# The product state @ w_in in another grouping: four batches in float32, four in high and low parts, each head in its own 64 rows of the array

## The chip, the cores and the metric

One core of a Trainium2 chip runs the kernel. The metric is the device time of one execution in microseconds (us). The engines meant below: PE (TensorE, matmuls; PEld its weight loads), DVE (VectorE), ACT (ScalarE), POOL (GpSimd) and SP (SyncE, whose queue issues the DMAs here). Each engine takes its instructions strictly in the order in which they stand.

## The reference

Softmax attention in both directions between x (8 batches, 8 heads, 512 tokens, 64 dims) and a small state (32 rows a head), then for all 8 x 544 rows a product, h - tanh(h), and a second product:

```python
scores = scale * x @ state.T;  a = softmax(scores);   xread = a @ state
scores2 = scale * state @ x.T; a2 = softmax(scores2); sread = a2 @ x
rows = concat([xread, sread], axis=tokens)      # (8 * 544, 512)
h = rows @ w_in                                 # w_in 512 x 2048
out = (h - tanh(h)) @ w_out                     # w_out 2048 x 512
```

The weights come as 8-byte floats and are made float32 on the chip.

## The kernel before

xread @ w_in is computed as a @ M with M = state @ w_in, per batch and head 32 x 2048 numbers. M is made on the chip, in four quarters q of w_in's columns (512 each), by pairs of heads p = 0 to 3 (one block of 128 rows of w_in).

The large products go through float32r: an operand is split exactly into hi + lo (`split`: ACT writes hi, DVE or POOL writes lo), and hi*hi + hi*lo + lo*hi are added up. A plain float32 matmul needs no split; in the trace it shows as two records.

The work goes by chunks: chunk i is batch i (512 tokens) for i < 8, chunk 8 holds the rows of sread. In a chunk, `hidden(f)` makes one of 16 column blocks of h (tile hps, from a's parts aT and M's parts m), then t = h - tanh(h) and g, the two parts of t; `output(f)` adds g's block into four output banks (tile ops; 12 matmuls a block, lines 393 to 395). `hidden` runs two blocks ahead of `output`. `load_m(b, q)` fetches a quarter of M (tile mr) and splits it into m.

M is made in three ways:

- `m_first_two(q, p)`, batches 0 and 1: one float32 matmul over all 128 rows. The two heads of a pair are laid out as a block matrix with zero halves (input sp, tile sps), so that one matmul gives both. Batch 0's part is copied straight into the tile mr, batch 1's goes to DRAM (tiles st, md).
- `m_units(0)`, batches 2 to 5: w's head of 64 rows is split, its hi stacked over its lo (tile wst, 64 rows each), and two float32r matmuls per head give all three products (state's lo and hi, each given twice, input sm).
- `m_units(1)`, batches 6 and 7: one matmul per head, with state's hi in half of the columns and its lo in the other half (input sl); two addends go to DRAM, and load_m adds them (tile ml).

The first quarter of batches 0 and 1 is made in a start sequence of its own, written out by hand. In the first chunk the float64 weights are converted as well (`convert_win`, `convert_wout`: DVE's lines 119 and 120, ACT's 122, POOL's 123), and the second batch's softmax is made.

The order on each engine is set by a scheduler that works on the program as written. What stands beside what in the program is set by the table SCH: for each kind of work (conversions "conv", m_first_two "pair", attention "att", m_units "m0", "m1", w_out "wo") the step (16 per chunk) at which each unit is written. PSUM banks for M, scores and transposes are two (pool ps_a). The raw tile mr has one buffer.

Of the kernel before, what the change touches and what calls it, by code (L numbers as in the profile page):

```python
# [31 lines left out]
def attention_ffn(ctx: ExitStack, tc: tile.TileContext, xT, xn, bd, sp, sm, sl, win, wout, xout, sout):  # L32
# [36 lines left out]
    # state @ w_in, [half of the heads, head, row, column]; of the last two batches, two addends  # L69
    mdram = [  # L70
        [[dram.tile([2, 4, NS, 512], F32, name=f"md{b}{q}{i}") for i in range(1 if b < 6 else 2)] for q in range(NQ)]
        for b in range(B)
    ]
# [13 lines left out]
    def split(hi, lo, src, sub=None):  # L87
        """src = hi + lo."""
        nc.scalar.copy(hi, src)  # L89
        return (sub or nc.vector).tensor_sub(lo, src, hi)  # L90

    class Weight:
        """A [P, 512] part of a weight: load() issues its load, convert() makes float32 of it."""
# [16 lines left out]
        def steps(self, dst):  # L110
            """convert() by engines: Vector's first and second part, Scalar's, GpSimd's."""
            if self.src.dtype == F32:
# [5 lines left out]
                # sign, the exponent's top bit; its other seven bits, 20 bits of the fraction  # L118
                lambda: nc.vector.tensor_scalar(u, high, 3, 0x3FFFFFFF, ALU.logical_shift_left, ALU.bitwise_and),  # L119
# [21 lines left out]
    def m_first_two(q, p):  # L141
        """Heads 2p and 2p + 1 of the first two batches, in float32 as it stands."""
        k, c = p // 2, p % 2
        if p == 0:
            # The first batch's part stays on chip.
            m_first[q] = pool.tile([P, 2, 512], F32, tag="mr", name=f"mr0{q}", bufs=RRB)
        ps = bank(ps_a, f"mps0{q}{p}")
        nc.tensor.matmul(ps, sps[:, p], wfs[q, k][:, c], start=True, stop=True)
        nc.scalar.copy(m_first[q][64 * c : 64 * c + 64, k], ps[0:64])
        stage = pool.tile([P, 2, 512], F32, tag="stage", name=f"st0{q}{p}", bufs=SB)  # L150
        nc.scalar.copy(stage[64:128, 0], ps[64:128])
# [4 lines left out]
    def m_units(g):
        """Of the next four batches (g = 0) and of the last two (g = 1), by pairs of heads.

        The columns of the last two batches' product: half of them by the state's hi, half by its lo.
        """  # L160
        raw = pool.tile([P, H, P], F32, tag="stage", name=f"smr{g}", bufs=SB)
        s = pool.tile([P, 2, H, P], F32R, tag="sm", name=f"sms{g}", bufs=1)
        if g == 0:
            nc.sync.dma_start(raw, sm)
            split(s[:, 0], s[:, 1], raw)
        else:
            nc.sync.dma_start(raw[:, :, 0:64], sl)
            split(s[:, 0, :, 0:64], s[:, 0, :, 64:128], raw[:, :, 0:64])
        for q in range(NQ):
            for k in range(2):  # L170
                w = pool.tile([P, 2, 512], F32, tag="wf", name=f"w1{g}{q}{k}", bufs=WB)
                nc.sync.dma_start(w, wf[q][:, 2 * k : 2 * k + 2])
                for c in range(2):
                    p = 2 * k + c
                    # Even heads: hi over lo; odd heads: lo over hi.
                    t = twins(f"wst{g}{q}{p}", [P, 2, 512], F32R)
                    split(t[0:64, 0], t[64:128, 0], w[0:64, c], WSUB)
                    split(t[64:128, 1], t[0:64, 1], w[64:128, c], WSUB)
                    hs = slice(2 * c, 2 * c + 2)
                    stage = pool.tile([P, 2, 512], F32, tag="stage", name=f"st{g}{q}{p}", bufs=SB)  # L180
                    for e in range(2):
                        h = 2 * p + e
                        ps = bank(ps_a, f"mps{g}{q}{h}")
                        if g == 0:
                            nc.tensor.matmul(ps, s[:, 1, h], t[:, e], start=True, stop=False)  # L185
                        nc.tensor.matmul(ps, s[:, 0, h], t[:, e], start=(g == 1), stop=True)  # L186
                        nc.scalar.copy(stage[:, e], ps)  # L187
# [517 lines left out]
```

## Time and profile before

| | |
|---|---|
| device time, median of 3 runs | 701.36 us (699.81 to 701.6) |
| span of the profiled execution, first to last instruction | 699.7 us; no other time of that execution is given |
| PE busy | 670.6 us (96%) |
| DVE busy | 464.8 us (66%) |
| ACT busy | 378.4 us (54%) |
| DMA moved | 99.68 MB, 142 GB/s over the span |

PE's busy share alone says little, since matmuls overlap at their ends: a float32r matmul is recorded at some 0.39 us while the next starts 0.23 us after it. What counts is the distance between starts, and whether PE waits.

### The profile page before, as it was taken

Reading aid. Unit: us, or ns where it says so; the run is one execution under the profiler, and the core shown is the slowest. Engines: PE = TensorE matmul, PEld = TensorE weight load, DVE = VectorE, ACT = ScalarE, POOL = GpSimd, SP = SyncE. Lnnn points to the kernel's source line nnn. Section 1 sums busy time; section 2 is a strip of 40 time slices with the busy share of each in tenths; the row PEclk is TensorE's granted clock in tenths of the full one; section 3 lists DMA queues with packets and bytes.
Section 4 is the critical chain, followed back from the end, with each engine's and each line's share of the span. In section 5 each row is a group of like instructions: output and inputs, shape, how many; then the busy total and the mean of one; then the engine's idle time right before and its main releaser. Section 6 shows DMA issues by size and latency. Waiting matters only on the chain.

```text
span 699.7 us, 8842 instructions
## 1 busy us (share of the span) xinstructions
PE 670.6 (96%) x3146; PEld 530.2 (76%) x3146; DVE 464.8 (66%) x755; ACT 378.4 (54%) x663; POOL 79.2 (11%) x59
## 2 busy tenths in 40 slices
PE   5888995999999999999999999999999999999997
PEld 2555663888778887888788878887888788888896
DVE  5998899965695559556776558545864596444442
ACT  3876866566674655447656545543543354333442
POOL 3766656200000000000000000000000000000000
PEclk9989899899999999999999999999999999999999
DMA  8887762553554554245635632563241312001400
GB/s 298 291 298 273 250 248 100 186 199 111 152 168 141 164 163 128 90 151 151 186 120 163 170 99 65 177 189 111 77 173 61 112 69 91 30 1 38 143 31 31
DMA packets 46316, 99.68 MB, mean 142 GB/s; under 512 B 6208, under 2 KB 12096, under 8 KB 46272
## 3 DMA queue, kind: packets, MB, share of 16 engines
q1 hardware_dynamic: 46272, 99.11, 43.9%
q8 instruction: 25, 0.41, 0.3%
q14 instruction: 19, 0.16, 0.1%
HBM read 67.11 MB, written 31.98 MB: 142 GB/s over the span
## 4 chain that ended last, share of the span: by engine, by line
PE 84%; DVE 9%; ACT 2%; issue 2%; POOL 1%; DMA 1%; SPq 0%; ACTq 0%; DVEq 0%; POOLq 0%
PE ops L395 17%; PE ops L393 17%; PE ops L394 16%; PE hps L356 9%; PE hps L355 9%; PE hps L357 8%; PE rps L309 2%; PE mps L186 2%; DVE w L120 2%; PE sps L249 2%; PE mps L185 1%; DMA w01d<-in_win 1%; PE pps L301 1%; DVE wor L119 1%; DVE w L119 1%
## 5 line engine op out<-in xcount | busy, mean ns | idle before, releaser
L393 PE MATMUL ops<-wo,g 128*128 128x512 f32 x544 | 211.1, 398 | 4.8 <-ACT wo L89 2.9
L394 PE MATMUL ops<-wo,g 128*128 128x512 f32 x544 | 215.1, 395 | 0.2 <-POOL wo L90 0.2
L395 PE MATMUL ops<-wo,g 128*128 128x512 f32 x544 | 208.9, 394 | 0.0
L363 ACT ACTIVATE t<-hps 128x512 f32<-128x512 f32 (+1 forms) x142 | 81.3, 573 | 151.3 <-PE hps L357 150.7
L363 DVE TENSOR_TENSOR t<-hps,t 128x512 f32<-128x512 f32 (+1 forms) x142 | 93.2, 658 | 102.3 <-ACT t L363 101.3
L393 PEld LDWEIGHTS ops<-wo,g 128*128 128x128 f32 x544 | 103.0, 190 | 32.7 <-ACT wo L89 4.6
L90 DVE TENSOR_TENSOR g<-t,g 128x512 fp32r<-128x512 f32 (+1 forms) x142 | 100.2, 706 | 39.9 <-ACT g L89 37.9
L89 ACT CAST g<-t 128x512 fp32r<-128x512 f32 (+1 forms) x142 | 84.7, 596 | 72.7 <-DVE t L363 69.8
L394 PEld LDWEIGHTS ops<-wo,g 128*128 128x128 f32 x544 | 103.0, 189 | 23.3 <-issue 2.3
L395 PEld LDWEIGHTS ops<-wo,g 128*128 128x128 f32 x544 | 103.4, 190 | 22.5 <-issue 0.5
L355 PE MATMUL hps<-aT,m 128*128 128x512 f32 x248 | 99.5, 402 | 3.3 <-DVE t L363 1.7
L357 PE MATMUL hps<-aT,m 128*128 128x512 f32 x248 | 98.4, 399 | 0.7 <-DVE m L90 0.7
L356 PE MATMUL hps<-aT,m 128*128 128x512 f32 x248 | 98.5, 398 | 0.0
L355 PEld LDWEIGHTS hps<-aT,m 128*128 128x128 f32 x248 | 47.3, 191 | 15.3 <-ACT m L89 2.4
L90 DVE TENSOR_TENSOR wst<-w,wst 64x512 fp32r<-64x512 f32 x64 | 46.0, 718 | 19.2 <-ACT wst L89 15.9
L356 PEld LDWEIGHTS hps<-aT,m 128*128 128x128 f32 x248 | 47.5, 191 | 11.7 <-issue 2.2
L357 PEld LDWEIGHTS hps<-aT,m 128*128 128x128 f32 x248 | 47.4, 191 | 11.7 <-DVE m L90 1.5
L90 DVE TENSOR_TENSOR m<-mr,m 128x1024 fp32r<-128x1024 f32 x31 | 39.9, 1287 | 9.4 <-ACT m L89 9.3
L187 ACT COPY st<-mps 128x512 f32<-128x512 f32 x64 | 36.7, 587 | 14.6 <-PE mps L186 14.3
L89 ACT CAST wst<-w 64x512 fp32r<-64x512 f32 x64 | 39.6, 619 | 2.3 <-issue 1.5
L89 ACT CAST m<-mr 128x1024 fp32r<-128x1024 f32 x31 | 32.3, 1042 | 3.6 <-DMA mr<-md 3.4
L90 POOL TENSOR_TENSOR wo<-wor,wo 128x512 fp32r<-128x512 f32 x16 | 25.3, 1586 | 6.0 <-ACT wo L89 6.0
(216 smaller groups left out, 661.7 us busy)
## 6 DMA issues: line engine op xcount, KB each, us to landing
md<-st SPq DMA_DIRECT2D x144, 128.0 KB, 2.3
mr<-md SPq DMA_DIRECT2D x28, 512.0 KB, 4.0
xT<-in_xT SPq DMA_DIRECT2D x16, 512.0 KB, 4.4
xn<-in_xn SPq DMA_DIRECT2D x16, 512.0 KB, 4.8
w<-wf SPq DMA_DIRECT2D x16, 512.0 KB, 4.9
out_x<-ob SPq DMA_DIRECT2D x32, 256.0 KB, 2.2
wn<-wf SPq DMA_DIRECT2D x8, 512.0 KB, 3.9
ml<-md SPq DMA_DIRECT2D x8, 512.0 KB, 3.6
```

The costliest lines, as they stand in the source:

```text
L89: nc.scalar.copy(hi, src)
L90: return (sub or nc.vector).tensor_sub(lo, src, hi)
L119: lambda: nc.vector.tensor_scalar(u, high, 3, 0x3FFFFFFF, ALU.logical_shift_left, ALU.bitwise_and),
L120: lambda: nc.vector.scalar_tensor_tensor(u, high, 0xC0000000, u, ALU.bitwise_and, ALU.bitwise_or),
L187: nc.scalar.copy(stage[:, e], ps)
L355: nc.tensor.matmul(ps, mhi[k][:, cols], ahi[:, k], start=(k == 0), stop=False)
L356: nc.tensor.matmul(ps, mhi[k][:, cols], alo[:, k], start=False, stop=False)
L357: nc.tensor.matmul(ps, mlo[k][:, cols], ahi[:, k], start=False, stop=(k == nk - 1))
L363: tanhs.append((nc.scalar.activation(t, ps, AF.Tanh).ins, nc.vector.tensor_sub(t, ps, t).ins))
L393: nc.tensor.matmul(o, g[:, 0, tok], wo[:, f, 0], start=(f == 0), stop=False)
L394: nc.tensor.matmul(o, g[:, 0, tok], wo[:, f, 1], start=False, stop=False)
L395: return nc.tensor.matmul(o, g[:, 1, tok], wo[:, f, 0], start=False, stop=(f == NFF - 1)).ins
```

## The change

Batches 0 to 3 now go through `m_first_four`: for each pair of heads two float32 matmuls, each over the 64 rows of its own head (rows 0 to 63 and 64 to 127 of the array), into two banks, with the four batches' 128 state rows as columns (input sf, second half of the tile sps). All of M goes through DRAM, batch 0's too; only the first quarter keeps its old way (batches 0 and 1 by the block matrix). Batches 2 and 3 of that first quarter, and batches 4 to 7 of all quarters, go through one `m_units`: w's 128 rows are split at once (one ACT and one DVE operation for a pair of heads), and each head gets three float32r matmuls over its 64 rows. Each pair's results leave in one write per batch (`pairs_out`). The two lists "m0", "m1" become one list "m".

```diff
-    def m_first_two(q, p):
...
-        ps = bank(ps_a, f"mps0{q}{p}")
-        nc.tensor.matmul(ps, sps[:, p], wfs[q, k][:, c], start=True, stop=True)
-        nc.scalar.copy(m_first[q][64 * c : 64 * c + 64, k], ps[0:64])
...
-        nc.sync.dma_start(mdram[1][q][0][k, 2 * c : 2 * c + 2].rearrange("h n f -> (h n) f"), stage[64:128, 0])
+    def pairs_out(q, p, ps, batches, name):
+        k, hs = p // 2, slice(2 * (p % 2), 2 * (p % 2) + 2)
+        n = NS * len(batches)
+        stage = pool.tile([P, 2, 512], F32, tag="stage", name=f"st{name}{q}{p}", bufs=SB)
+        for e in range(2):
+            nc.scalar.copy(stage[:n, e], ps[e][:n])
+        for j, b in enumerate(batches):
+            nc.sync.dma_start(mdram[b][q][k, hs].rearrange("h n f -> n h f"), stage[NS * j : NS * j + NS])
+
+    def m_first_four(q, p):
+        ps = [bank(ps_a, f"mps0{q}{p}{e}") for e in range(2)]
+        for e in range(2):
+            rs = slice(64 * e, 64 * e + 64)
+            nc.tensor.matmul(ps[e], sps[rs, 1, p], wfs[q, p // 2][rs, p % 2], start=True, stop=True)
+        pairs_out(q, p, ps, range(4), "f")

-    def m_units(g):
...
-                    split(t[0:64, 0], t[64:128, 0], w[0:64, c], WSUB)
-                    split(t[64:128, 1], t[0:64, 1], w[64:128, c], WSUB)
...
-                        if g == 0:
-                            nc.tensor.matmul(ps, s[:, 1, h], t[:, e], start=True, stop=False)
-                        nc.tensor.matmul(ps, s[:, 0, h], t[:, e], start=(g == 1), stop=True)
+    def m_units():
...
+        for batches in (range(2, 4), range(4, 8)):
...
+            for q in range(1 if n < P else NQ):
...
+                        split(t[:, 0], t[:, 1], w[:, c], WSUB)
+                        ps = [bank(ps_a, f"mps{n}{q}{p}{e}") for e in range(2)]
+                        for i, (x, y) in enumerate(((1, 0), (0, 1), (0, 0))):
+                            for e in range(2):
+                                rs = slice(64 * e, 64 * e + 64)
+                                nc.tensor.matmul(
+                                    ps[e][:n], s[rs, x, p, cols], t[rs, y], start=(i == 0), stop=(i == 2)
+                                )
+                        pairs_out(q, p, ps, batches, f"g{n}")

     def load_m(b, q):
-        if b == 0:
-            r = m_first[q]
...
-                nc.vector.tensor_add(r, r, r2)
+        r = pool.tile([P, 2, 512], F32, tag="mr", name=f"mr{b}{q}", bufs=RRB)
+        nc.sync.dma_start(r, mdram[b][q].rearrange("g h n f -> (h n) g f"))
...
-    SCH = ... "m0": [11, 11, 15, 15, 20, 21, ..., 35, 36], "m1": [40, 46, 52, ..., 79, 84], ...
+    SCH = ... "m": [9, 10, 11, 13, 34, 35, ..., 52, 54], ...
```

In the order of instructions the change shows at three places. The lines of the changed file stand 15 to 17 lower: its L154 is the float32 matmul of m_first_four, L178 the float32r one of m_units, L338 to L340 are `hidden`, L376 to L378 `output`, L346 makes t, L87 is split's subtraction, L116 and L117 are the conversions.

First, PE in the first chunk, where its second quarter (hps0_4, q = 1) begins. Before (mps02.. are pairs of q = 2):

```order
L394 MATMUL ops0_3_392<-wo_77,g0_2_345 128x512
L395 MATMUL ops0_3_392<-wo_77,g0_2_345 128x512
L355 MATMUL hps0_4_497<-aT0_124,m01_494 128x512
L356 MATMUL hps0_4_497<-aT0_124,m01_494 128x512
L355 MATMUL hps0_5_548<-aT0_124,m01_494 128x512
L356 MATMUL hps0_5_548<-aT0_124,m01_494 128x512
L148 MATMUL mps020_562<-w020_468,sps_126 128x512
```

After, at the same place (behind g0_2), and then where hps0_4 now stands:

```order
L377 MATMUL ops0_3_399<-wo_77,g0_2_347 128x512
L378 MATMUL ops0_3_399<-wo_77,g0_2_347 128x512
L154 MATMUL mps0131_440<-w011_323,sps_118 128x512
L284 MATMUL pps01_461<-ident_72,s01_154 128x128 x4
L154 MATMUL mps0200_575<-w020_480,sps_118 128x512
L154 MATMUL mps0201_576<-w020_480,sps_118 128x512
L376 MATMUL ops0_0_396<-wo_77,g0_3_436 128x512
```

```order
L154 MATMUL mps0220_597<-w021_536,sps_118 128x512
L154 MATMUL mps0221_598<-w021_536,sps_118 128x512
L154 MATMUL mps0230_608<-w021_536,sps_118 128x512
L154 MATMUL mps0231_609<-w021_536,sps_118 128x512
L338 MATMUL hps0_4_511<-aT0_116,m01_508 128x512
```

The last half that hps0_4's quarter needs (mps0131, pair 3 of q = 1) stands behind g0_2's products, and hps0_4 moved behind all four pairs of the next quarter.

Second, DVE in the first chunk, where the third quarter's t and g come (t0_8, g0_8). Before:

```order
L120 SCALAR_TENSOR_TENSOR wor6_663<-wo6d_611,wor6_663 128x512
L119 TENSOR_SCALAR wor7_723<-wo7d_619 128x512
L363 TENSOR_TENSOR t0_8_743<-hps0_8_736,t0_8_743 128x512
L363 TENSOR_TENSOR t0_9_792<-hps0_9_785,t0_9_792 128x512
L120 SCALAR_TENSOR_TENSOR wor7_723<-wo7d_619,wor7_723 128x512
L90 TENSOR_TENSOR g0_8_746<-t0_8_743,g0_8_746 128x512
```

After (wst6400 and wst6401 are the first units of batches 2 and 3, e10 and at10 the second batch's softmax):

```order
L87 TENSOR_TENSOR wst6400_1011<-w16400_1009,wst6400_1011 128x512
L257 TENSOR_TENSOR e10_739<-e10_739,z10_869 128x512
L87 TENSOR_TENSOR wst6401_1073<-w16400_1009,wst6401_1073 128x512
L346 TENSOR_TENSOR t0_8_787<-hps0_8_780,t0_8_787 128x512
L259 STREAM_TRANSPOSE at10_874<-e10_739 128x512
L116 TENSOR_SCALAR wor15_1162<-wo15d_917 128x512
L346 TENSOR_TENSOR t0_9_841<-hps0_9_834,t0_9_841 128x512
L87 TENSOR_TENSOR g0_8_790<-t0_8_787,g0_8_790 128x512
```

t0_8 moved from between the conversions of w_out's blocks 6 and 7 to the last one, 15, and behind the first splits for batches 2 and 3.

Third, PE in chunk 3, at one of the last units for batches 4 to 7. Before, the two heads of a unit of batches 6 and 7 stand side by side in the full array:

```order
L357 MATMUL hps3_6_2747<-aT3_2201,m31_2694 128x512
L186 MATMUL mps104_2768<-wst102_2762,sms1_2289 128x512
L186 MATMUL mps105_2771<-wst102_2762,sms1_2289 128x512
L393 MATMUL ops3_0_2651<-wo_77,g3_4_2707 128x512
L394 MATMUL ops3_0_2651<-wo_77,g3_4_2707 128x512
```

After (mps128231 is the second head of one unit, mps128300 the first head of the next):

```order
L340 MATMUL hps3_6_2794<-aT3_2079,m31_2723 128x512
L178 MATMUL mps128231_2609<-wst12823_2605,sms_1006 128x512 x3
L338 MATMUL hps3_6_2794<-aT3_2079,m31_2723 128x512
L339 MATMUL hps3_6_2794<-aT3_2079,m31_2723 128x512
L178 MATMUL mps128300_2665<-wst12830_2662,sms_1006 128x512 x3
L340 MATMUL hps3_6_2794<-aT3_2079,m31_2723 128x512
```

Here each head's three matmuls stand alone between others; in the ten units ahead of these, the two heads' matmuls stand next to each other.

More of the change, by code (lines that the diff above doesn't have):

```diff
@@ L68, in attention_ffn @@
     sr = [cpool.tile([P, DM], F32, name=f"sr{g}") for g in range(2)]
[L70 to L73, printed above, removed]
+    mdram = [[dram.tile([2, 4, NS, 512], F32, name=f"md{b}{q}") for q in range(NQ)] for b in range(B)]
     wf = [dram.tile([P, 4, 512], F32, name=f"wf{q}") for q in range(NQ)]
@@ L156, in m_units @@
-    def m_units(g):
-        raw = pool.tile([P, H, P], F32, tag="stage", name=f"smr{g}", bufs=SB)
-        s = pool.tile([P, 2, H, P], F32R, tag="sm", name=f"sms{g}", bufs=1)
-        if g == 0:
[L164 to L176, printed above, removed]
-                    split(t[0:64, 0], t[64:128, 0], w[0:64, c], WSUB)
-                    split(t[64:128, 1], t[0:64, 1], w[64:128, c], WSUB)
[L179 to L187, printed above, removed]
-                    for j in range(4):
-                        dst = mdram[2 + j][q][0] if g == 0 else mdram[6 + j % 2][q][j // 2]
-                        nc.sync.dma_start(dst[k, hs].rearrange("h n f -> n h f"), stage[32 * j : 32 * j + 32])
-                    yield
@@ new lines, in m_first_four @@
+    def m_first_four(q, p):
[5 more added lines that the diff above has]
+    def m_units():
+        raw = pool.tile([P, 4, 6 * NS], F32, tag="stage", name="smr", bufs=SB)
+        nc.sync.dma_start(raw, sm)
+        s = pool.tile([P, 2, 4, 6 * NS], F32R, tag="sm", name="sms", bufs=1)
+        split(s[:, 0], s[:, 1], raw)
+        for batches in (range(2, 4), range(4, 8)):
+            n = NS * len(batches)
+            cols = slice(NS * (batches[0] - 2), NS * (batches[0] - 2) + n)
+            for q in range(1 if n < P else NQ):
+                for k in range(2):
+                    w = pool.tile([P, 2, 512], F32, tag="wf", name=f"w1{n}{q}{k}", bufs=WB)
+                    nc.sync.dma_start(w, wf[q][:, 2 * k : 2 * k + 2])
+                    for c in range(2):
+                        p = 2 * k + c
+                        t = twins(f"wst{n}{q}{p}", [P, 2, 512], F32R)
+                        split(t[:, 0], t[:, 1], w[:, c], WSUB)
[7 more added lines that the diff above has]
+                        pairs_out(q, p, ps, batches, f"g{n}")
+                        yield
@@ L536, in step @@
             for p in range(4):
-                o(nc.tensor.matmul(mps[j][:, p], sps[:, p], w[:, p], start=True, stop=True))
+                o(nc.tensor.matmul(mps[j][:, p], sps[:, 0, p], w[:, p], start=True, stop=True))
         elif k == "k":
@@ L592, in attention_ffn @@
         load(1)
-        m_first_two(1, p)
+        m_first_four(1, p)
     first = afters[FILL[3]]
-    m1 = [m_units(g) for g in range(2)]
+    units = m_units()
     atts = {}
-    SCH = dict(json.loads('{"conv": [0, 1, 2, 2, 3, 3, 4, 4, 6, 7], "pair": [0, 1, 3, 3, 3, 3, 4, 5, 6, 7], "a0": [0, 0, 1, 13], "att0": [3, 5, 7, 7, 7, 8, 9, 11, 13], "att1": [6, 7, 8, 8, 11, 11, 11, 11, 13], "att2": [5, 9, 9, 13, 13, 13, 13, 13, 13], "m0": [11, 11, 15, 15, 20, 21, 21, 22, 22, 23, 25, 27, 29, 33, 35, 36], "m1": [40, 46, 52, 53, 53, 54, 55, 57, 62, 62, 62, 65, 73, 77, 79, 84], "wo": [0, 1, 2, 3, 4, 5, 6, 7, 8, 8, 9, 9, 10, 10, 12]}'))
+    SCH = dict(json.loads('{"conv": [0, 1, 2, 2, 3, 3, 4, 4, 6, 7], "pair": [0, 1, 3, 3, 3, 3, 4, 5, 6, 7], "a0": [0, 0, 1, 13], "att0": [3, 5, 7, 7, 7, 8, 9, 11, 13], "att1": [6, 7, 8, 8, 11, 11, 11, 11, 13], "att2": [5, 9, 9, 13, 13, 13, 13, 13, 13], "m": [9, 10, 11, 13, 34, 35, 36, 37, 38, 40, 41, 42, 43, 44, 46, 47, 48, 50, 52, 54], "wo": [0, 1, 2, 3, 4, 5, 6, 7, 8, 8, 9, 9, 10, 10, 12]}'))
     D0 = dict(
@@ L607, in attention_ffn @@
         },
-        m0=list(range(17, 33)),
-        m1=list(range(48, 80, 2)),
         wo=list(range(0, 15)),
@@ L647, in attention_ffn @@
             for _ in range(D0["pair"].count(st)):
-                m_first_two(*next(pairs))
+                m_first_four(*next(pairs))
             with tc.issue_after(first):
@@ L656, in attention_ffn @@
                     advance(atts[b], n)
-            for g in range(2):
-                advance(m1[g], D0[f"m{g}"].count(st))
+            advance(units, D0["m"].count(st))
             chunks[i].output(f)
@@ L682 @@
     sp = sp.reshape(P, 4, P)
[L684 to L686 removed]
+    sf, sm = (
+        c(t.reshape(len(t), 4, 2, D, NS).transpose(2, 3, 1, 0, 4).reshape(P, 4, -1)) for t in (sT[:4], sT[2:])
     )
```

29 lines of the change are left out of this document (6 added, 23 removed).

## The prediction

> **What bounds the kernel now.** I read the busy shares first, then a table by stage, then the instructions at the seam between the stages. The page's 40 slices:
>
> ```profile
> PE   5888995999999999999999999999999999999997
> DVE  5998899965695559556776558545864596444442
> PEclk9989899899999999999999999999999999999999
> ```
>
> VectorE (DVE) is at 8 or 9 tenths up to the seventh slice (122 us); PE dips there to 5 and is full from the ninth slice on. By stage (us; busy time of PE, its weight loads, DVE, ScalarE, GpSimd; clock; DMA share; GB/s):
>
> ```profile
> 20.00:40.00 20.00, 14.95 (x52) 7.81 (x50) 19.76 (x30) 17.01 (x33) 14.76 (x10) 0.99 0.84 274
> 40.00:60.00 20.00, 19.18 (x78) 13.66 (x79) 17.98 (x23) 15.29 (x27) 14.05 (x11) 0.84 0.89 299
> 60.00:80.00 20.00, 16.78 (x56) 11.74 (x55) 18.63 (x22) 13.57 (x24) 12.40 (x8) 0.83 0.64 231
> 80.00:100.00 20.00, 20.00 (x83) 13.63 (x82) 17.55 (x24) 15.35 (x27) 13.88 (x11) 1.00 0.81 286
> 100.00:120.00 20.00, 13.95 (x69) 9.89 (x68) 19.24 (x28) 14.06 (x24) 10.68 (x7) 1.00 0.38 138
> 142.00:690.00 548.00, 548.00 (x2645) 445.50 (x2644) 338.09 (x574) 282.03 (x493) 0.00 (x0) 1.00 0.38 118
> ```
>
> Two stages, then. To about 122 us DVE (weight conversions) leads and PE follows with gaps. From 142 to 690 us PE is busy 548.00 of 548 us at full clock, so there each microsecond of PE time counts whole, and DVE's 338 and ScalarE's 282 are under cover: the smaller number of splits, copies and loads of the change is worth nothing there. The seam:
>
> ```profile
> 118.14 0.39 PE L186 MATMUL mps<-wst,sms 128*128 128x512 f32 x1
> 122.18 0.80 PE L185 MATMUL mps<-wst,sms 128*128 128x512 f32 x1 [3.65 <-DVE sr L315]
> 122.77 0.63 PE L186 MATMUL mps<-wst,sms 128*128 128x512 f32 x1
> 123.20 0.63 PE L355 MATMUL hps<-aT,m 128*128 128x512 f32 x1
> 142.66 0.39 PE L355 MATMUL hps<-aT,m 128*128 128x512 f32 x1
> ```
>
> PE's last long wait ends with DVE's sr at 122.18; then matmuls stand 0.43 apart (122.77, 123.20) where they otherwise stand 0.23 apart, for the 5 to 6 us that PE's clock takes to come back: 13 of them, 2.6 us lost. At 142.66 all of the first chunk, and hps_0 and hps_1 of the second, is done.
>
> **Prices on PE.**
>
> ```profile
> 261.63 0.39 PE L394 MATMUL ops<-wo,g 128*128 128x512 f32 x1
> 263.90 0.39 PE L357 MATMUL hps<-aT,m 128*128 128x512 f32 x1
> ...
> 188.90 0.39 PE L355 MATMUL hps<-aT,m 128*128 128x512 f32 x1
> 189.22 1.08 PE L249 MATMUL sps<-xT,bdr 128*64 128x512 f32 x4
> 190.23 0.50 PE L356 MATMUL hps<-aT,m 128*128 128x512 f32 x1
> 190.56 0.39 PE L185 MATMUL mps<-wst,sms 128*128 128x512 f32 x1
> ...
> 265.13 1.94 PE L249 MATMUL sps<-xT,bdr 128*64 128x512 f32 x8
> ...
> 88.77 1.02 PE L148 MATMUL mps<-w,sps 128*128 128x512 f32 x2
> 89.86 0.40 PE L394 MATMUL ops<-wo,g 128*128 128x512 f32 x1
> ...
> 213.18 0.39 PE L395 MATMUL ops<-wo,g 128*128 128x512 f32 x1
> 213.50 1.09 PE L309 MATMUL rps<-xn,p2t 128*64 128x128 f32 x16
> 214.52 0.66 PE L301 MATMUL pps<-ident,s 128*128 128x128 f32 x4
> 214.94 0.71 PE L355 MATMUL hps<-aT,m 128*128 128x512 f32 x2
> ```
>
> Ten float32r matmuls from 261.63 to 263.90: 0.227 us each. A float32 one of L148 with the L393 behind it takes 89.86-88.77 = 1.09, so 0.86 alone. No matmul before uses half of the array's rows; the nearest rows are L249, which uses half of its columns. Eight records (four matmuls, two records each) last 1.94, four last 1.08: two more float32 matmuls cost 0.86, the price of one. Halves do run side by side. But going over costs: from 188.90 to 190.56 are 1.66 us, less two float32r (0.45) and the 0.86 leave **0.35 us per excursion** into a half mode and back. For half rows I bound it by 0 and 0.35 and take 0.35, the only half mode in the trace. rps and pps in the last four rows cost 1.1 (1.34 less 0.23) and 0.4.
>
> **Term 1, after 142 us.** Before, 84 of the 96 float32r matmuls of L185 and L186 stand there: 84 x 0.227 = 19.1 us. After, 16 units for batches 4 to 7 of six half-row matmuls each. The order tells which halves stand together: in three units they alternate (3 steps), in seven they go two, two, one, one (4 steps, since the second half can run beside the first's last ones), in six each half's three stand alone. 9 + 28 + 36 = 73 steps x 0.227 = 16.6 us. They make 10 excursions in the ten joined units and 11 in the six others: 21 x 0.35 = 7.35. Sum 23.9, so **+4.8 us**; with free excursions -2.5.
>
> **Term 2, the first 142 us.** Batch 0's product now goes through DRAM. Before, hps_4 begins right after g_2's products:
>
> ```profile
> 51.59 0.39 PE L355 MATMUL hps<-aT,m 128*128 128x512 f32 x1
> ...
> L151 ACT COPY st<-mps 64x512 f32<-64x512 f32 x12 | 7.0, 582 | 0.3
> L89 ACT CAST m<-mr 128x1024 fp32r<-128x1024 f32 x31 | 32.3, 1042 | 3.6 <-DMA mr<-md 3.4
> ...
> md<-st SPq DMA_DIRECT2D x24, 128.0 KB, 3.6
> mr<-md SPq DMA_DIRECT2D x3, 512.0 KB, 4.0
> ```
>
> After, the last half that it needs (mps0131) takes that place; then come 0.86 matmul, 0.58 copy, 3.6 write, 4.0 read, 1.04 cast and about 0.9 to issue both DMAs: 62.6, 11 us later. PE has four pairs and g_3 to fill this, so the delay itself is half covered; but DVE's order has been turned round with it, conversions first: g_8 now follows wo14 and the second batch's softmax. When? DVE reached sr at 120.97:
>
> ```profile
> 109.51 0.68 DVE L90 TENSOR_TENSOR wst<-w,wst 64x512 fp32r<-64x512 f32 x1
> 110.95 0.69 DVE L90 TENSOR_TENSOR wst<-w,wst 64x512 fp32r<-64x512 f32 x1
> 117.45 3.48 DVE L90 TENSOR_TENSOR wst<-w,wst 64x512 fp32r<-64x512 f32 x2
> 120.97 1.16 DVE L315 TENSOR_SCALAR sr<-rps,ri 32x64 f32<-32x64 f32 x4
> 122.16 0.69 DVE L363 TENSOR_TENSOR t<-hps,t 128x512 f32<-128x512 f32 x1
> 122.76 0.68 DVE L90 TENSOR_TENSOR g<-t,g 128x512 fp32r<-128x512 f32 x1
> 124.63 0.42 DVE L119 TENSOR_SCALAR wor<-wo15d 128x512 uint32<-128x512 uint32 x1
> ```
>
> DVE operations of 512 columns follow each other 0.60 apart (122.16, 122.76). Up to sr, after has one conversion more (1.1: 0.42 and 0.68 for its two halves) and less: four half splits (4.85) for two whole ones (1.3, some 0.65 each), two m splits (2.4), t_12 (0.6), small ones and a shorter sms (0.7). That is 6.1 us less: sr at 114.8. Fourteen rows lie between g_8 and sr, twelve of 0.6, sms 0.95: g_8 is done at 106.6. DVE thus gains six microseconds, but PE cannot begin ops_8 before 106.6, and behind it, counted in the order, stand 66 float32r matmuls up to hps_14 (15.0), 12 half ones of the new units, all alone (2.7), 4 excursions (1.4), rps 1.1, pps 0.4: 127.2. Then 72 more up to the place reached before at 142.66 (16.3), 12 half ones (2.7), 4 excursions (1.4), two rps (2.0): 149.6. **+6.9 us.** Not counted, because PE waits there anyway: the 13 excursions and three unpaired halves of the float32 pairs (13 x 0.35 + 3 x 0.86 = 7.1 us). Bounds of this term: if nothing waits on DRAM and DVE's 6.1 and the 2.6 at half speed come through, less ten more matmuls (2.3), -6.4; if none of the 7.1 is hidden, +14.0. I keep +6.9, which the order gives.
>
> **Term 3, the queues.** SP now issues four writes a pair for one, and 512 KB are read three times more: 12 x 3 x 128 KB and 1.5 MB, 6.3 MB in a stage that moved 21.8 MB from 20 to 100 us at a mean share of 0.80. It fits if the loads of w_out slide into 100 to 120 us (share 0.38). I take 0; if it doesn't fit, 6.3 MB at 280 GB/s are 22 us, of which the 0.2 free (16 us) take most: +6.
>
> Sum: 699.7 + 6.9 + 4.8 = 711.4. The page gives that execution no other time than its span of 699.7; the median of the runs stands 1.7 above it, the lowest 0.1. I say **711.5 us**, its own range 706 to 717.
>
> **Rivals.**
> *Faster: the switch is cheap and DVE's relief arrives.* For it: DVE does 6.1 us less and PE's 3.65 us wait and slow 5 us may go. Against it: 0.35 in every L249 excursion, and the order puts g_8 behind the conversions. With free excursions term 1 is -2.5 and term 2, if it goes half of the way from 4.1 (6.9 less its eight excursions) to its lower bound, about -1: 696. It decides at the excursion: with 29 of them on the path (21 and 8), the full relief (-8.9 in all with term 1) is used up at 0.31 us each. Chance 0.20; another 0.08 for ending within 0.3% of before.
> *Half rows don't run side by side* though half columns do: the ten joined units need 60 steps for 37, 5.2 us more: 716.7. Chance 0.10.
> *Weight loads show.* In three half matmuls in a row, the second and third load weights into rows that are still at work. If that isn't hidden, 24 loads after 142 us and 16 before, of 0.19 each:
>
> ```profile
> L186 PEld LDWEIGHTS mps<-wst,sms 128*128 128x128 f32 x64 | 12.2, 190 | 2.8 <-issue 0.5
> ```
>
> 7.6 us, so 719. Against it: in the full array these loads of 0.19 lie beside the running matmul of the same rows, and the step stays 0.227. The Trainium skill ("TensorE: Matmul & The Clock Gate", Part 3) says that weight loads overlap running matmuls only where the row groups differ; by it the sum would be 719, but this trace's full-array rows disagree with it. Chance 0.05.
> *DMA and SP are too full* (term 3, with weights late): 717. Chance 0.15.
> The forecast itself: 0.42. That nothing of this is done can't be: the order shows the half-row matmuls.
>
> **How the numbers follow.** Slower: 0.42 + 0.10 + 0.05 + 0.15 = 0.72; faster 0.20; same 0.08 (0.3% is about 2 us, what a measurement of this kernel can tell from no change). The range leaves out 1 in 10 at each end: half of the faster cases lie under 697, and over 720 what adds two of the slower rivals. 697 to 720.
>
> **What would show it.** Right: hps_4 some 10 us later than 51.6; DVE's g_8 near 105 and PE short of work before it; the first chunk done near 150; matmuls of L178 in lone threes with gaps of about 0.1 on each side. Wrong: matmuls on either side of L178 0.23 apart, or PE full from before 110 us.

## The result, and the profile after

The kernel after takes 722.88 us (median of 4 runs, 721.72 to 723.53), the kernel before 700.59 on the same chip (4 runs, 699.74 to 701.6). The ratio is 1.0317 with a 95% interval of 1.0300 to 1.0334: slower by 22 us, where 711.5 was forecast and 720 was the end of the range. The span of the profiled execution went from 699.7 to 721.7 us.

I cut both executions at one place of the program, the first matmul of hps_2 of the second chunk, and call it the seam. In the kernel before it stands at 142.66 us; here it is in the kernel after (timeline of PE: start, length, engine, line, operation, tiles):

```profile
159.21 0.39 PE L378 MATMUL ops<-wo,g 128*128 128x512 f32 x1
159.44 0.39 PE L338 MATMUL hps<-aT,m 128*128 128x512 f32 x1
```

Up to the seam the change costs 16.8 us (6.9 forecast). Behind it stand 721.7 - 159.4 = 562.3 us against 699.7 - 142.7 = 557.0: **5.2 us** (4.8 forecast). The second half of the forecast came out, the first did not.

The 40 slices of the page of the kernel after:

```profile
PE   5885889999999999999999999999999999999997
DVE  5976989557465447653475448544854395444452
PEclk9998987999999999999999999999999999999999
DMA  9899956452113455553532202220231022000310
```

PE is full from the seventh slice on (108 us). On the way there PE falls to 5 tenths and DVE to 6 in the same slice, the fourth (54 to 72 us), where before both stood at 8: in this place no engine leads. By stretches (us; busy time of PE, weight loads, DVE, ACT, POOL; granted clock; DMA share; GB/s):

```profile
40.00:60.00 20.00, 17.95 (x73) 10.49 (x72) 14.96 (x21) 10.25 (x18) 13.16 (x10) 0.91 0.98 325
60.00:80.00 20.00, 10.69 (x29) 5.68 (x27) 14.50 (x15) 11.00 (x19) 13.60 (x11) 0.74 1.02 378
80.00:100.00 20.00, 19.35 (x75) 12.55 (x76) 17.14 (x18) 13.24 (x23) 15.26 (x11) 1.00 0.87 299
100.00:120.00 20.00, 17.60 (x45) 9.89 (x44) 18.93 (x32) 12.04 (x23) 10.40 (x7) 0.66 0.51 159
160.00:712.00 552.00, 552.00 (x2653) 437.82 (x2652) 298.61 (x522) 241.75 (x423) 0.00 (x0) 1.00 0.28 90
```

From 60 to 80 us PE works 10.7 of 20 us while the DMA engines are full (share 1.02); from 100 to 120 us its clock is 0.66. The last row says that behind the seam PE is the bound as before: 552.00 of 552 us.

The same view over the whole first stage, from 0 to the seam, for the kernel before

```profile
0.00:142.66 142.66, 117.27 (x474) 80.36 (x475) 125.83 (x179) 94.53 (x165) 79.24 (x59) 0.92 0.71 242
```

and for the kernel after:

```profile
0.00:159.44 159.44, 131.47 (x511) 81.31 (x511) 122.02 (x177) 93.08 (x166) 77.55 (x59) 0.90 0.76 256
```

This is the row to read for every run below. The same products of hps are done at its end. DVE's work shrank by 3.8 us, but its idle time rose from 16.8 to 37.4. PE is busy 14.2 us more (busy time by clock: 131.5 x 0.90 = 118 us for 117.3 x 0.92 = 108), and **it still waits 28.0 us (159.44 - 131.47), as against 25.4 before**. The forecast had put the pairs' added time into those waits. But of the 25.4 us, 9.5 end with the first load of x and the first weight conversions, before 24 us, and the first pair begins at 31.6: they were no room for the pairs. PE's waits, first of before, then of after (who waited for whom: us in total, times, longest):

```profile
PE mps L537 <- POOL w L123: 4.9, 3, 3.1
PE sps L497 <- DMA xT<-in_xT: 4.6, 1, 4.6
```

```profile
PE mps L154 <- ACT stf L144: 11.4, 5, 5.1
```

The pairs' own groups, before and after (count, busy us, mean ns of a record, idle time before them and what ended it):

```profile
L148 PE MATMUL mps<-w,sps 128*128 128x512 f32 x24 | 12.5, 609 | 3.0 <-ACT st L151 1.6 <-POOL w L123 1.4
```

```profile
L154 PE MATMUL mps<-w,sps 64*128 64x512 f32 x48 | 21.7, 717 | 13.3 <-ACT stf L144 11.4
```

9.2 us more of busy time, and 10.3 us more of waiting right before them: 11.4 of the 13.3 us end with ACT's copies into the stage buffer. The longest of these waits (5.1 us, ended at 69.83) was for a copy that stood on ACT behind a cast of w_out, for which ACT itself waited for POOL:

```profile
68.58 0.62 ACT L86 CAST wo<-wor 128x512 fp32r<-128x512 f32 x1 [3.88 <-POOL wor L120]
69.11 1.06 ACT L144 COPY stf<-mps 128x512 f32<-128x512 f32 x2
```

From 40 to 160 us ACT waited 13.6 us in all for POOL before such casts; before the change 5.5 us (40 to 142 us).

### The profile page after: what moved, and what is told of

Its sections match the earlier page's. It is cut to its first block, busy times and chain, and to the rows that moved or that the text cites. A ratio compares the mean times of both kernels' runs of the same rounds, so it can differ in the third digit from the quotient of the medians.

```text
span 721.7 us, 8724 instructions
## 1 busy us (share of the span) xinstructions
PE 689.7 (96%) x3194; PEld 524.2 (73%) x3194; DVE 422.2 (58%) x702; ACT 337.0 (47%) x594; POOL 77.6 (11%) x59
## 4 chain that ended last, share of the span: by engine, by line
PE 85%; DVE 5%; DMA 4%; ACT 2%; issue 1%; POOL 1%; SPq 1%; ACTq 0%; POOLq 0%; DVEq 0%
PE ops L376 17%; PE ops L377 17%; PE ops L378 17%; PE hps L340 9%; PE hps L338 9%; PE hps L339 9%; PE mps L178 3%; PE rps L292 2%; PE sps L232 2%; PE pps L284 1%; DMA w01d<-in_win 1%; DMA wo8d<-in_wout 1%; DVE w L117 1%; DMA w31d<-in_win 1%; DMA wo13d<-in_wout 1%
## 5 line engine op out<-in xcount | busy, mean ns | idle before, releaser
L376 PE MATMUL ops<-wo,g 128*128 128x512 f32 x544 | 214.3, 398 | 0.6 <-ACT wo L86 0.6
L378 PE MATMUL ops<-wo,g 128*128 128x512 f32 x544 | 208.5, 393 | 0.0
L346 DVE TENSOR_TENSOR t<-hps,t 128x512 f32<-128x512 f32 (+1 forms) x142 | 93.4, 659 | 158.0 <-ACT t L346 157.1
L346 ACT ACTIVATE t<-hps 128x512 f32<-128x512 f32 (+1 forms) x142 | 81.4, 574 | 201.2 <-PE hps L340 200.8
L376 PEld LDWEIGHTS ops<-wo,g 128*128 128x128 f32 x544 | 102.7, 189 | 31.5 <-issue 3.7
L87 DVE TENSOR_TENSOR g<-t,g 128x512 fp32r<-128x512 f32 (+1 forms) x142 | 98.3, 694 | 44.3 <-ACT g L86 42.0
L378 PEld LDWEIGHTS ops<-wo,g 128*128 128x128 f32 x544 | 102.4, 188 | 25.3 <-issue 4.2
L338 PE MATMUL hps<-aT,m 128*128 128x512 f32 x248 | 99.7, 402 | 2.3 <-DVE t L346 2.2
L340 PE MATMUL hps<-aT,m 128*128 128x512 f32 x248 | 99.2, 402 | 0.1
L338 PEld LDWEIGHTS hps<-aT,m 128*128 128x128 f32 x248 | 47.5, 191 | 18.5 <-DVE t L346 4.9
L340 PEld LDWEIGHTS hps<-aT,m 128*128 128x128 f32 x248 | 47.8, 193 | 14.3 <-issue 2.9
L87 DVE TENSOR_TENSOR m<-mr,m 128x1024 fp32r<-128x1024 f32 x31 | 38.6, 1246 | 11.2 <-ACT m L86 10.6
L144 ACT COPY stg<-mps 128x512 f32<-128x512 f32 (+1 forms) x40 | 22.4, 586 | 28.7 <-PE mps L178 25.3
L154 PE MATMUL mps<-w,sps 64*128 64x512 f32 x48 | 21.7, 717 | 13.3 <-ACT stf L144 11.4
L87 DVE TENSOR_TENSOR wst<-w,wst 128x512 fp32r<-128x512 f32 x20 | 14.7, 734 | 28.9 <-ACT wst L86 28.9
L178 PE MATMUL mps<-wst,sms 64*128 64x512 f32 (+1 forms) x120 | 27.0, 423 | 0.0
```

The costliest lines, as they stand in the source:

```text
L144: nc.scalar.copy(stage[:n, e], ps[e][:n])
L154: nc.tensor.matmul(ps[e], sps[rs, 1, p], wfs[q, p // 2][rs, p % 2], start=True, stop=True)
L178: nc.tensor.matmul(ps[e][:n], s[rs, x, p, cols], t[rs, y], start=(i == 0), stop=(i == 2))
L338: nc.tensor.matmul(ps, mhi[k][:, cols], ahi[:, k], start=(k == 0), stop=False)
L340: nc.tensor.matmul(ps, mlo[k][:, cols], ahi[:, k], start=False, stop=(k == nk - 1))
L346: tanhs.append((nc.scalar.activation(t, ps, AF.Tanh).ins, nc.vector.tensor_sub(t, ps, t).ins))
```

## Experiments

Each run is read at the same seam; a profile is one execution and can lie up to 2 us off the median of the timed runs, so both are given. The scheduler orders each program anew, so the number of other matmuls ahead of the seam varies too: c and h have 6 fewer there than after, some 1.4 us at 0.227 each, and a has 20 fewer than before, so a's seam (138.4) is not used. Times of before beside them were 700.25 to 700.94.

### One burden at a time

Three things were added to the first stage: writes, batch 0's way through DRAM, and time of the pairs on PE.

```diff
 # a_more_writes, on before, after the write of batch 1
+        for x in range(3):
+            nc.sync.dma_start(more[q][x, k, 2 * c : 2 * c + 2].rearrange("h n f -> (h n) f"), stage[64:128, 0])
 # b_batch0_dram, on before
-        nc.scalar.copy(m_first[q][64 * c : 64 * c + 64, k], ps[0:64])
+        nc.scalar.copy(stage[0:64, 0], ps[0:64])
+        nc.sync.dma_start(mdram[0][q][0][k, 2 * c : 2 * c + 2].rearrange("h n f -> (h n) f"), stage[0:64, 0])
...
 # c_batch0_chip, on after: two small copies, no write or read of batch 0
+            nc.scalar.copy(m_first[q][64 * c + 32 * e : 64 * c + 32 * e + 32, k], ps[e][0:32])
+        pairs_out(q, p, ps, range(4), "f", 1)
...
 # d_half_writes, on after
+        for j, b in list(enumerate(batches))[: 2 if name == "f" else 4]:
...
```

> The kernel before, with three more writes of 128 KB after each of the twelve float32 pairs, into memory that nobody reads (4.7 MB, of the 6.3 MB that the change adds). The third chunk-1 product hps_2 starts at 142.7 us before and 159.4 after. If the full DMA engines alone make the missing 10 us (T1), it starts at 150 to 156 here, the pairs' waits on the stage copies grow from under 1 us to several, and the time is 708 to 714. If the traffic fits into the free share, as the prediction took it (term 3 at zero), or if it is the order (T2) or batch 0's way through DRAM (T3), it starts at 142 to 144 and the time is 700 to 702.

> The kernel before, with batch 0's product written to DRAM and read back as the change does, everything else as before (12 writes and 3 reads more, 3.0 MB). If the round trip makes the whole shift of the first stage (T3), hps_2 of chunk 1 starts at 155 or later and the time is 712 to 717. By the prediction's own term 2 (the round trip delays hps_4 by 10 us, half of it covered) 146 to 150, time 704 to 708. If the bytes are what counts (T1), half of the 6.3 MB: 148 to 151. If the round trip is under cover: 142 to 144, 700 to 702.

> The kernel after, with batch 0's product kept on the chip by two more copies of 32 rows a pair on ScalarE; the other three batches are written as before (3.0 MB less traffic). If the round trip makes the shift (T3): hps_4 starts near 52 to 55 us, hps_2 of chunk 1 at 143 to 147, time 705 to 709. If it is the bytes (T1): half of them are left, hps_2 of chunk 1 at 150 to 154, time 712 to 716. If it is the order of DVE with g_8 behind the conversions (T2): 156 or later, 719 or more.

> The kernel after without the float32 pairs' writes of batches 2 and 3 (3.1 MB less); their chunks read the product of batches 0 and 1 instead, so this part of the computation is left out. Batch 0 still goes through DRAM. If the bytes make the shift (T1): hps_4 starts at 63 to 66 instead of 72.2, hps_2 of chunk 1 at 150 to 153, time 712 to 716. If it is the round trip (T3) or the order (T2): hps_4 at 70 or later, hps_2 of chunk 1 at 157 to 160, time 720 to 723.

Measured: a 700.25 us (ratio to before 0.9998, 0.9984 to 1.0012); b 703.27 (1.0041, 1.0028 to 1.0054); c 725.34 (seam 162.2); d 721.37 (1.0241 to 1.0349, seam 159.5). The writes alone cost the kernel before nothing, though they fill the DMA engines (view by stretches of a, 60 to 80 us):

```profile
60.00:80.00 20.00, 18.84 (x73) 13.18 (x72) 19.47 (x23) 14.36 (x24) 11.40 (x9) 1.00 0.95 326
```

b is the sharper result. There hps_4 begins at 65.82 us instead of 51.59, 14 us later where the forecast had 11, and g_8 is split at 103.17 instead of 81.81, and yet the seam moves by 1.6 us and the time by 3.0:

```profile
0.00:144.26 144.26, 115.70 (x475) 76.89 (x476) 124.81 (x179) 95.75 (x168) 80.44 (x59) 0.94 0.77 261
```

A late hps_4 and a late g_8 are thus mostly covered by other work, and so is the turned order of DVE that goes with them: in b 27 of DVE's 32 conversions of w_out stand ahead of g_8, where before has 16 and after 31. So, alone, full DMA engines (a, T1) and the round trip (b, T3) are not the cause. On the other side c and d gave nothing back, 1.5 us at most. c is a weak test, though: it puts two more copies a pair on ACT, and hps_4 still came at 67.72 where 52 to 55 was expected. In d the pairs waited less (5.7 us for the stage copies), but PE then waited 6.5 us at hps_4 (70.27) for batch 0's part of M, which still came through DRAM.

### Time on PE

```diff
 # f_top_pairs, on after
+            nc.tensor.matmul(ps[e], top(sps[rs, 1, p]), top(wfs[q, p // 2][rs, p % 2]), start=True, stop=True)
 # g_before_double, on before
+        for _ in range(2):
+            nc.tensor.matmul(ps, sps[:, p], wfs[q, k][:, c], start=True, stop=True)
 # o_two_banks, on before: the second matmul into a bank of its own, batch 1 copied from there
+        for e in range(2):
+            nc.tensor.matmul(pss[e], sps[:, p], wfs[q, k][:, c], start=True, stop=True)
...
 # z_bank_only: as o, the second matmul with operands top(...), one pass
```

> The kernel after, with the 24 float32 half-row matmuls of the pairs fed by the upper 16 bits of their operands, so that each takes one pass of the array instead of four; the product loses that precision. Transfers, copies and the round trip stay. The four runs before moved bytes and the round trip and left the seam (start of chunk 1's hps_2) where it was, and TensorE's idle time before it lies between 23 and 29 us in all six kernels. New theory T4: the pairs' time on TensorE is on the path, nothing of it is covered by TensorE's waits. A block of a pair or a lone half falls from 1.2 to 0.6 us with its excursion; 15 blocks: 9 to 10 us less, seam at 148 to 151 instead of 159.4, time 711 to 715. If TensorE's waits cover the pairs (the prediction's step), the seam stays at 157 to 160 and the time at 720 to 723.

> The kernel before, with each of the twelve float32 pair matmuls issued twice (the second overwrites the first): 12 x 0.86 = 10.3 us more on TensorE in the first stage, nothing else. If TensorE's waits of 25 us there cover it (the prediction's step), the seam stays at 142 to 145 and the time at 700 to 703. If the pairs' time is on the path (T4): seam at 150 to 154, time 708 to 712.

> The kernel before with each pair's float32 matmul made twice, into two PSUM banks, one for each of its two copies; batch 0 stays on chip, one write a pair. Doubled into one bank it took 7.5 us more. If the second bank is what the sum of the parts missed: 709.5 to 711, TensorE's waits for the stage copies several us. If not: 707 to 709.

> The kernel before, with batch 1's half of each pair taken from a second matmul in one pass (upper 16 bits of the operands, precision lost) into a bank of its own: 12 x 0.23 = 2.7 us more on TensorE, and two banks a pair. If the second bank costs what o took over g: 702 to 704. If it costs nothing and only TensorE's time counts: 701 to 702.5. If it is what holds s (8 us): 707 or more.

Measured: g 707.89 us (1.0108, 1.0082 to 1.0134), o 710.32 (1.0151, 1.0118 to 1.0184), z 703.32 (1.0035, 1.0022 to 1.0049); f 724.57. The first stage of g:

```profile
0.00:148.29 148.29, 123.97 (x498) 82.50 (x499) 120.59 (x179) 96.05 (x168) 77.60 (x59) 0.94 0.71 233
```

10.3 us of matmuls that do nothing cost 7.5 us (the seam 5.6), although PE waited 25.4 us in that stage; it still waits 24.3. That is the step of the forecast, tried by itself: **the waits took up about a quarter of the time added on PE, not all of it.** Since ACT's copies wait for the second matmul, g lengthens the chain of each pair together with PE's work; matmuls that nobody waits for were not tried. A second bank a pair seems to cost some 2.4 us more (o against g, whose intervals overlap; in z it takes 2.4 us together with 2.7 us on PE). But f falls the other way:

```profile
0.00:161.92 161.92, 122.44 (x486) 78.57 (x487) 124.76 (x177) 92.25 (x166) 77.70 (x59) 0.88 0.77 253
```

PE is busy 9 us less than in the kernel after, and waits 39.5 us instead of 28.0. So PE's time alone (T4) isn't the cause in the kernel after either. What stood behind it is the way of batch 0's part through DRAM: hps_4 begins when it does in the kernel after (72.23), only that PE now waits there for the cast of m:

```profile
72.01 0.80 PE L341 MATMUL hps<-aT,m 128*128 128x512 f32 x1 [7.96 <-ACT m L86]
```

### All burdens at once

m puts everything on the kernel before (two matmuls and two banks a pair, four writes, batch 0 through DRAM); j takes three things off the kernel after.

```diff
 # m_before_sum, on before: o, b, and two writes more a pair to memory that nobody reads
 # j_three_off, on after: f and c, and
+        pairs_out(q, p, ps, range(2), "f", 1)
+        nc.sync.dma_start(r, mdram[1 if b in (2, 3) and q > 0 else b][q].rearrange("g h n f -> (h n) g f"))
...
 # e_stage3, on after
-    SB = int('2')
+    SB = int('3')
```

> The kernel before with all burdens of the new first stage at once, and its late part untouched: each pair's float32 matmul is made twice, into a bank of its own for each of its two copies; four writes a pair, two of them to memory nobody reads; batch 0's product through DRAM. Alone, these gave: writes 0, round trip 3.0 us, doubled matmul 7.5 us. If the burdens add up (T5): 10 to 11 us, time 710 to 712, seam 150 to 153. If they multiply one another as in the kernel after, where taking one away gave nothing back: seam 156 to 160, time 714 to 719. If it is only the order that the scheduler made there (T2): less than 10 us.

> The kernel after with three burdens taken away at once: pairs' matmuls in one pass (upper 16 bits of the operands, precision lost), batch 0 kept on chip, and no writes of batches 2 and 3 by the pairs (their chunks read batch 1's product: that part of the computation is left out). Alone, none of the three moved the seam from 159.4 by more than 3 us. If several chains are about equally long and each alone was caught by the next (T5): seam 144 to 149, time 706 to 711. If the order of the instructions holds the seam whatever they take (T2): seam 156 or later, time 718 or more.

> The kernel after with three stage buffers instead of two, so that the copies of a pair need not wait for the writes of the pair but one before. ScalarE's stage copies released 11.4 us of TensorE's waits. If the recycling of that buffer is a link of the longest chain: seam at 152 to 156, time 715 to 719. If the two PSUM banks of a pair or other chains hold it: seam 157 to 160, time 720 to 724.

Measured: m 713.49 us (1.0183, 1.0162 to 1.0203), j 715.12, e 720.70 (1.0281, 1.0266 to 1.0296). The first stage of m:

```profile
0.00:154.66 154.66, 124.65 (x499) 80.46 (x499) 122.00 (x179) 95.89 (x168) 76.44 (x59) 0.97 0.79 264
```

Seam +12.0, time +12.8: with no half rows and the late part untouched, the burdens make about three quarters of the 16.8 us. The time lies between the two ranges that were expected, since o had not been run then; with it, the burdens simply add up (0 from a, 3.0 from b, 9.9 from o). j, also between its two ranges, gives 9.3 us back in the seam, though its parts gave nothing alone. The third stage buffer is worth 2 us.

### The late part, and what is left of the first stage

```diff
 # h_alternate, on after: each unit's matmuls held in the written order
+                                if i or e:
+                                    tc.keep_in_program_order(mm)
 # i_late_stacked, on after: batches 4 to 7 in the form of before
+                        nc.tensor.matmul(ps[e], s[:, 1, 2 * p + e], t[:, e], start=True, stop=False)
+                        nc.tensor.matmul(ps[e], s[:, 0, 2 * p + e], t[:, e], start=False, stop=True)
...
 # n_all_stacked: as i, and batches 2 and 3 of the first quarter too
 # l_late_chip3: i, c and e;  q_stacked_stage3: n and e
 # s_all_off: n and j
 # y_two_copies: s, with the write of batch 1 taken from the tile of batch 0, no stage copies
```

> The kernel after, with batches 4 to 7 in the form of before: high and low part stacked over the 128 rows, four whole-array float32r matmuls a pair of heads, no excursion. 64 x 0.227 = 14.5 us for 23.9: the part behind the seam takes 553 us, the time is 712 to 715. If row halves cost what whole rows cost and the 5.2 us behind the seam come from elsewhere: 720 or more. The seam itself stays at 157 to 161.

> The kernel after, with the six half-row matmuls of each late unit held in the written order, row halves alternating. By the prices of the prediction (0.227 us a step, 0.35 us an excursion) the sixteen late units fall from 73 steps and 21 excursions (23.9 us) to 48 steps and 16 excursions (16.5): the part behind the seam takes 555 us instead of 562.3, the time is 714 to 717. If only the excursions count (halves do not share the array in float32r): 27.4, the part behind the seam 566, time 726. If the halves' order makes no difference: 722 to 724.

> The kernel after with batches 4 to 7 stacked over the whole array (time 711.7 alone, the part behind the seam 551.9), batch 0 kept on the chip, and three stage buffers. If the round trip and the buffer are what keep the seam late: seam 146 to 150, time 699 to 704, which would be level with before or better. If the other chains hold it: seam 157 to 162, time 711 to 715.

> As i_late_stacked (711.7), with the four early units (batches 2 and 3, first quarter) stacked over the whole array too: no float32r half-row matmul is left. In the kernel after these 24 half matmuls stand in eight blocks of 7.7 us; stacked, 16 x 0.227 = 3.6. TensorE is full from about 104 us on, so if their time counts whole (T6): seam 4 us earlier than i's 158.0, at 153 to 155, time 706.5 to 709. If the first stage ends with other chains: seam 157 to 159, time 711 to 713.

> n_all_stacked with three stage buffers. The third buffer gave the kernel after 2 us (722.9 to 720.7). If it gives that here too: 2 us under n_all_stacked, 704 to 707, still above before's 700.5. If the buffer's chain is caught by others: equal to n_all_stacked within 1 us.

> n_all_stacked with the three burdens of j_three_off taken away as well (pairs in one pass of the upper 16 bits, batch 0 on chip, no pair writes of batches 2 and 3; their chunks read batch 1's product). If pairs, round trip and early half-row units are the whole of the 16.8 us: seam at 142 to 147, part behind it 552, time 695 to 700. If a part of the 16.8 us is none of these (the order that the scheduler made): seam 149 or later, 703 or more.

> s_all_off with two copies a pair on ScalarE instead of four and no stage buffer: the write of batch 1 takes its data from the tile that holds batch 0's product (so this part of the computation is left out). TensorE's work stays at 106 us. If copies and buffers hold the seam: 142 to 146, time 694 to 699. If the second bank or the order does: 149 or later, 701 or more.

Measured, with the seam and the part behind it (span less seam) from the profile:

| | time, us | ratio, 95% | seam | behind it |
|---|---|---|---|---|
| before | 700.59 | | 142.7 | 557.0 |
| after | 722.88 | 1.0300 to 1.0334 | 159.4 | 562.3 |
| h | 723.71 | 1.0303 to 1.0358 | 156.1 | 565.7 |
| i | 711.66 | 1.0148 to 1.0179 | 158.0 | 551.9 |
| l | 714.03 | 1.0178 to 1.0226 | 158.6 | 553.0 |
| n | 712.85 | 1.0139 to 1.0192 | 159.7 | 551.8 |
| q | 707.76 | 1.0084 to 1.0130 | 152.5 | 552.2 |
| s | 706.88 | 1.0054 to 1.0124 | 151.0 | 552.8 |
| y | 698.04 | 0.9946 to 0.9974 | 141.8 | 553.8 |

*i* shows term 1: without half rows the part behind the seam is 10.4 us shorter (9.4 expected), the seam 1.5.

*h* was expected to gain 7.4 us and gained none. In the kernel after the scheduler had put the six matmuls of ten late units side by side, and left the threes of the others alone:

```profile
257.91 0.39 PE L376 MATMUL ops<-wo,g 128*128 128x512 f32 x1
258.23 0.96 PE L178 MATMUL mps<-wst,sms 64*128 64x512 f32 x6
259.13 0.50 PE L377 MATMUL ops<-wo,g 128*128 128x512 f32 x1
...
354.76 0.39 PE L377 MATMUL ops<-wo,g 128*128 128x512 f32 x1
355.08 0.96 PE L178 MATMUL mps<-wst,sms 64*128 64x512 f32 x3
355.98 0.50 PE L378 MATMUL ops<-wo,g 128*128 128x512 f32 x1
```

Six in alternate halves and three in one half take the same time, 0.96 us for the group. Held in the written order, most units fall apart into one and five, with ops between them (timeline of h). That the second half's bank comes free later would explain it; this was not looked into.

```profile
249.24 0.39 PE L380 MATMUL ops<-wo,g 128*128 128x512 f32 x1
249.55 0.50 PE L178 MATMUL mps<-wst,sms 64*128 64x512 f32 x1
249.98 0.49 PE L378 MATMUL ops<-wo,g 128*128 128x512 f32 x1
250.41 0.96 PE L178 MATMUL mps<-wst,sms 64*128 64x512 f32 x5
251.30 0.50 PE L379 MATMUL ops<-wo,g 128*128 128x512 f32 x1
```

Counted over both traces behind 165 us, the 96 late half matmuls stand in 21 blocks in the kernel after and in 29 in h. What the blocks add to the distance of their neighbours, summed, is 22.9 us there and 25.5 here, so h's part behind the seam should be 2.6 us longer; measured are 3.4, of which 1.4 come from the 6 matmuls that moved behind the seam. The number of excursions decides: by the steps alone, 63 there and 61 here, h would gain.

*n* tried whether the early half-row units (eight blocks, 7.7 us; stacked 3.6) are what m lacks. The seam did not come earlier, so this theory (T6) fell as stated: PE's busy time stayed (129.8 us for i's 130.1), with a lower clock (0.88 for 0.91) and 2 us more waiting. With the third stage buffer (q) the seam then came 7.2 us earlier (the time 5.1), more than that buffer gave the kernel after (3.2, the time 2.2).

*s and y* look at the scheduler's order (T2). s, with every burden off, still stood at 151.0. But to keep batch 0 on the chip it makes two small copies a pair besides the two stage copies. y drops the stage copies. ACT's groups and the first stage, of s

```profile
L144 ACT COPY stf<-mps 128x512 f32<-128x512 f32 x24 | 13.9, 583 | 0.3
L159 ACT COPY mr<-mps 32x512 f32<-32x512 f32 x24 | 13.8, 574 | 4.7 <-DVE m L87 3.8 <-PE mps L158 0.5
```

```profile
0.00:151.01 151.01, 118.65 (x477) 76.12 (x477) 123.62 (x177) 106.64 (x189) 79.09 (x59) 0.90 0.68 223
```

and of y:

```profile
L159 ACT COPY mr<-mps 32x512 f32<-32x512 f32 x24 | 13.8, 573 | 2.4 <-DMA md<-mr 1.1 <-PE mps L158 0.8
```

```profile
0.00:141.77 141.77, 113.09 (x476) 74.97 (x477) 123.59 (x176) 95.37 (x168) 77.98 (x59) 0.93 0.71 238
```

Dropping the stage copies, 13.9 us on ACT, gave 9.2 us of seam, and y's first stage ends where that of before does (142.66). y drops their buffer with them, but ACT had hardly waited ahead of these copies (0.3 us in all in s), so the buffer held little. So with these burdens and copies gone, nothing else in the program holds the seam late. y isn't a test of the turned order of DVE, since its g_8 stands behind 18 of the 32 conversions, nearly as before; b is that test, with 3.0 us. y also suggests why c and l gave nothing in the seam and j no more than it did, since they make the same 24 copies besides. y leaves work out, so its 698.04 us is no result to use; no run that computes the whole in full precision beat the kernel before.

## Why the prediction was right and wrong

- **Term 1, +4.8 us behind the seam: right**, 5.2 measured (in c, d, e, f and j, with the same late part, 4.0 to 6.2). The mechanism is that of the forecast; that the sum came so close is in part luck, since two errors offset each other: 63 steps and not 73, and an excursion some 0.41 us and not 0.35, together 22.9 us for the 23.9 forecast.
- **Half rows side by side, weight loads hidden: right.** The lone threes and the alternate sixes take the same 0.96 us. The Trainium skill ("TensorE: Matmul & The Clock Gate", Part 3) says in one sentence that loads overlap only where the row groups differ, by which the threes would be longer, and in another that a load into the background weight buffer is pulled ahead too; the trace agrees with the second.
- **Term 2, +6.9 us: wrong, 16.8.** The step that failed is "Not counted, because PE waits there anyway" (7.1 us of excursions and unpaired halves). g tried that cover by itself: of 10.3 us added on PE, 7.5 came out, and the waits stayed at 24.3. They were no slack: 9.5 of the 25.4 us lay ahead of the first pair, and in the kernel after the pairs brought waits of their own, 11.4 us for ACT's stage copies. Split by the clock as above, after is over before by 10 us of PE's work at full clock, 4 us of lower clock and 3 us of waiting, so the waits took up none of the added work, they grew beside it. Even the upper bound, +14.0 with none of the 7.1 hidden, was too low.
- **The path that term 2 did count was the wrong one.** Its delay was real in place: hps_4 came at 72.23 (62.6 forecast):

```profile
54.32 1.75 SPq L146 DMA_DIRECT2D md<-stf  x4
...
63.49 0.38 SPq L186 DMA_DIRECT2D mr<-md  x1
...
70.06 1.06 ACT L86 CAST m<-mr 128x1024 fp32r<-128x1024 f32 x1
...
72.23 0.79 PE L338 MATMUL hps<-aT,m 128*128 128x512 f32 x1
```

  The read was issued 7.4 us after the last of these writes; 2.9 us of that are the write's landing (at 58.93), and behind it weight loads and the next pair's writes stood ahead of the read in SP's queue. From there it took 6.6 us to the cast (4.0 forecast). g_8 came at 113.90 (106.6). But no wait of PE ends with it, though the forecast's sum lets PE wait for it. PE's last wait ends at 102.77, and from there to the seam PE is busy all the time, first at half clock:

```profile
102.77 1.81 PE L154 MATMUL mps<-w,sps 64*128 64x512 f32 x2 [2.17 <-ACT stf L144]
```

```profile
102.77:159.44 56.67, 56.44 (x241) 37.20 (x241) 41.03 (x72) 32.51 (x58) 10.17 (x7) 0.88 0.49 149
```

  This is also the sign that the forecast had named for being wrong, PE full from before 110 us. And b shows that such delays alone cost 1.6 us of seam and 3.0 of time: the 6.9 was a plausible sum from the wrong link.
- **"DVE gains 6.1 us": wrong.** DVE did 3.8 us less work and idled 20.6 us more. "DVE leads" was read from its busy share; in the kernel after it no longer led.
- **Small slips:** 711.4 us is a span, and a time lies some 1.8 us above it (723.53 with 721.7), so the forecast should have said 713. Of the fourteen rows between g_8 and sr it prices thirteen. In the slices of before, PE is full from the eighth on, not the ninth.
- **Term 3, 0 for the writes: right alone** (a: 0.9998). In company it is not clear: taking half of the writes off the kernel after gave 1.5 us (d, two runs that lie 2.1 us apart), a third stage buffer 2.
- **The rivals:** the faster one fell; "DMA and SP too full" (717) saw part of it (full engines at 60 to 80 us, the read behind others on SP) but not PE's share. In the kernel after the chain that ended last goes through three loads of weights on its way from 56 to 89 us:

```profile
56.18 5.99 DMA w31d<-in_win
70.96 6.15 DMA wo8d<-in_wout
83.56 5.60 DMA wo13d<-in_wout
```

  Before, the first load of all is the only one in that chain up to the seam. Yet d's chain has none of the three either, and d's first stage ends at the same place (159.5): chains of about the same length stand beside one another here.
- **Open:** m reproduces 12.0 of the 16.8 us, and by another split than the kernel after: over before, 13 us more of work at full clock, 6 us less lost by the clock, 5 us more of waiting. The other 4.8 go with a lower clock (0.90 for m's 0.97; busy time by clock is 118 us in the kernel after and 121 in m, so it is no added work). Whether the clock is their cause isn't shown: over the whole execution it was 0.978 in after and 0.992 in m, and in the runs of before a like difference (0.979 for 0.993) went with some 1.4 us. The early half-row units were the obvious reason, and n did not show it.

## What to carry to other kernels

An engine's waits in a stage that nobody leads are not room for more work: before pricing an added matmul at nothing, ask when each wait falls and what ends it, and try it by issuing the matmul twice. Where taking away one burden gives nothing back, put them all on the kernel before, together and singly; the sum is easier to read there than from the side of the kernel after. A split of the array by rows is paid by the excursion, so what counts is how many blocks the order leaves, and pinning the order can make more of them.

## What the runs showed of the hardware that I had not expected

- Six float32r matmuls in alternate row halves and three in one half take the same 0.96 us as a group; a block costs three steps of 0.227 and some 0.41 us around it.
- A DMA share of 0.95 from 60 to 80 us (0.64 before), with 4.7 MB of added writes, cost the kernel before nothing measurable (ratio 0.9998, 0.9984 to 1.0012).
- Dropping 24 copies of 0.58 us on ACT, which was busy 106.6 of 151.0 us, gave 9.2 us in the first stage (s against y; their buffer went with them).
